# Three neighbouring chunks in one load: regrouping the cache loads of a two-layer decode kernel

## The chip, the cores and the metric

The kernel runs on one core of a Trainium2 chip. The metric is the device time of one execution in microseconds (us). Three runs of the kernel before gave 2494.72, 2493.18 and 2493.18 us, a median of 2493.18 us.

## What is computed

The reference is one decode step (one token for each of B = 2 sequences, D = 512 channels) through two layers that share all their weights and caches:

```python
x = x + A(layernorm(x))   # attention over a cache of 32768 tokens, 32 query heads on 8 KV heads, Dh = 128
x = x + B(layernorm(x))   # token mixer: W2 gelu(W1 layernorm(X)^T), with F = 1792 hidden values
x = x + A(layernorm(x))   # the same K and V caches a second time
x = x + B(layernorm(x))
```

For each sequence and KV head, four query rows are multiplied with 32768 keys, a softmax is taken, and its weights are multiplied with 32768 values. Everything is in 32-bit floats. K and V of both sequences are 537 MB, and each layer needs all of it, while the on-chip memory that the kernel uses for it holds about 28 MB. The second layer's queries of a sequence depend on the whole first layer of that sequence, the mixer included.

## The kernel before

**Units, chunks, cells.** A unit is one (layer, sequence, KV head): 32 units, numbered 0 to 31 in the order of the list `units`. K and V of a unit are cut into 8 chunks each (c0 to c7) of 4096 tokens. A chunk is 128 partitions by 4096 floats, 16 KB in each partition and 2 MB in all. One tile, `mem`, holds 13 cells of this size (0 to 12) and a rest of 5/8 of a cell (called cell 13). Chunks c0 to c3 of a unit, and c4 to c7, lie next to each other in every row of DRAM, so that one load can take several neighbouring chunks, with rows of 16 KB times their number. Far from the layer changes four chunks come in a load (64 KB rows) and the eight cells 0 to 7 are used in two groups of four.

**The order of the work.** The list `stream` (L858 to L869) sorts all loads by a key, so that K chunks of unit n+1 alternate with V chunks of unit n. The final loop (L1008) goes through it: it issues the load, then emits the matmuls of each chunk (`k_chunk`, L422: 16 instructions in two halves of 8; `v_chunk`, L567: the same), then the small work that was booked with `at(step, ...)` for this step. A step is one chunk; half steps (`vend + 0.5`) lie between the two halves of a chunk. TensorE (PE) executes in exactly this order. All cache and weight loads are issued by SyncE (its queue, SPq), in order: a load waits there until the last reader of its cells has finished, and every load behind it waits too. A matmul waits until the whole load that brought its chunk has landed.

**Which cell.** The choice is made when the program is built. `hold` notes until which step a cell is in use, `room` and `fit` say how many cells' worth of loads were issued since its last reader, and `spread` takes the cell with the most room; where there is less than two it cuts the chunk into two half loads of 1 MB (8 KB rows), for which `half` takes half cells with a room of at least one.

**What stays.** Head 7 (the `keeper`) is processed in layer 0 and layer 1 of a sequence without a second load of all of it: `KEPT_K` and `KEPT` name the K chunks (c0 to c2) and V chunks (c1 to c7, of c4 only 5/8, and two more eighths in PSUM) that layer 0 leaves in cells of their own until layer 1 has read them. So when a sequence changes from layer 0 to layer 1, the chunks kept can be worked on without a load. Units 13 (layer 0, sequence 0, head 7; N1) and 16 (layer 0, sequence 1, head 7; N2) are loaded into these cells; units 15 and 18 (N3) read them again. Units 14 and 17 (head 5 of the other sequence) run in between.

**A layer change.** After the last V chunk of unit 13 (or 16; its end is `vend`) comes a chain of small work: `out_0` (VectorE adds the blocks of `acc`), `out_1` and `out_2` (PE, L607 and L240), `take_rows`, `mix_2` (PE, L653), `hidden_sum` (14 gelu tiles on ScalarE, 14 sums on VectorE), `mix_3` (PE, L817), `to_columns`, and then the query products of the next unit. `mix_1` (PE, L629) is booked one step before `vend`. Meanwhile the loads go on with K chunks c2 to c7 of unit 14 (17), then V c0 and on. Nearly all cells are held by then, so these come as half loads in a ring of four half cells: the first half of c4 goes where the first half of c2 was, the first half of c5 where that of c3 was, the second halves likewise.

**Weights.** `load_weights` (L113) brings `wq` and `wo` of one head, 2 MB in 16 KB rows, into one of the cells 9 to 12, ten steps ahead of the first unit that needs them: 8 loads in layer 0, 6 in layer 1 (head 5 and 7 stay).

The functions that the change touches, with their lines:

Of the kernel before, what the change touches and what calls it, by code (L numbers as in the profile page):

```python
# [13 lines left out]
P = 128  # L14
CK = 4096
JT = CK // P
NG = 4
# [4 lines left out]
LAG = 1  # L22


KEPT_K = {0: 0, 1: 1, 2: 9}
KEPT = {1: (8, 6), 2: (8, 2), 3: (8, 11), 4: (5, 13), 5: (8, 3), 6: (8, 4), 7: (8, 5)}
REST = 5
IN_PSUM = (4, 5, 2)
KEPT_Q = 4
RESIDENT = (5, 7)  # L30
PAIRS = (2, 4, 7)
EVEN = 6
PIECES = (32, 16, 8, 4, 4)
THIN = 16
QT = 4
# [7 lines left out]
def gqa_mixer_kernel(ctx: ExitStack, tc: tile.TileContext, x, kt, v, wqo, cols, out):  # L43
# [20 lines left out]
    DH = D // NG  # L64
    NCH = kt.shape[1] // (CK * DH)
    HKV = U // B
    R = wqo.shape[2] // (2 * D)
    DT = D // P
    FT = (cols.shape[1] - 1) // 4
    LAYERS = 2  # L70
# [22 lines left out]
    nc.scalar.dma_start(xcols, x)  # L93


    W = wqo.shape[2] // 2
    assert CK == 2 * W
    WCELL0, WCELLS = RING * RING, 4
    heads = list(range(HKV))
# [10 lines left out]
    def wo_at(h):  # L110
        return cells(home[h])[:, W:].rearrange("p (t c) -> p t c", t=R)

    def load_weights(h, cell):  # L113
        home[h] = cell
        nc.sync.dma_start(cells(cell), wqo[h])


    busy = [0] * 2 * (WCELL0 + WCELLS + 1)
# [19 lines left out]

    def buffer(m, limit, until):

        ks = range(0, limit - m + 1, m) if limit != EVEN else [k + j for k in PAIRS for j in range(0, 2, m)]
        k = min(ks, key=lambda k: (-room(k, m, until), idle(k, m)) if limit == NCH else idle(k, m))
        assert idle(k, m) <= now[0]
        hold(k, m, until)
        return cells(k, m)
# [7 lines left out]

    def fit(k, m, until):

        return 0 if until > closed.get(int(k), until) else room(k, m, until)

    def room(k, m, until):

# [4 lines left out]

        return sum(brings[int(-(-a // 1)) : b])

    def spread(until, parted=False):

        k = min((*range(WCELL0 + 1), KEPT[3][1]), key=lambda k: (-fit(k, 1, until), idle(k)))
        if fit(k, 1, until) >= 2 and not parted:  # L170
            hold(k, 1, until)
            return [cells(k)]
        return [half(until - 0.5), half(until)]

    def quads(a):
# [213 lines left out]
    def load_k(n, c, m, limit):  # L389
        layer, b, h = unit_of(n)  # L390
        stay = h == keeper and c in KEPT_K
        own = KEPT_K[c] if stay else None
        until = k_done[n, c + m - 1]
        if own is not None:
            if stay and not layer:
                until = k_done[units.index((1, b, h)), c + m - 1]
            hold(own, m, until)
            bufs = [cells(own, m)]
        elif limit == RING:
            bufs = spread(until, n in (N1 + 1, N2 + 1) and c > 1)  # L400
# [89 lines left out]
    def load_v(n, c, m, limit):  # L490
        layer, b, h = unit_of(n)
        src = piece(v, b * HKV + h, c, m)
        stay, own = stays(n, c)
        until = v_done[n, c + m - 1]
        w = QT * DH
        f = stay * w
        at = quads(own) if stay else []
        if stay:
            if layer == 0:
                load(own, src[:, :f])  # L500
                for j in range(2 if stay > QT else 1):
                    busy[2 * KEPT[c][1] + j] = v_done[units.index((1, b, h)), c]
            if stay == JT // QT:
                v_at[n, c] = at
                return
            bufs = [half(until)[:, : CK - f]]
        elif limit == RING:
            bufs = spread(until)
# [47 lines left out]
    def v_chunk(n, c, part):  # L556
# [7 lines left out]
        for q in range(part * NG, min(quads, (part + 1) * NG)):  # L564
            g = q % NG
            col = (c2 * (JT // QT) + q) * 32 + a * R * QT
            nc.tensor.matmul(  # L567
                acc[32 * g : 32 * g + R * QT, :],
                S[half][:, col : col + R * QT],
                vc[q],  # L570
                start=(c == 0 and q < NG),
                stop=(c == NCH - 1 and q >= quads - NG),
            )
        if part < SUB - 1:
# [283 lines left out]
    stream = []  # L858
    for n in range(NU):
        stream += [(n * NCH + c + m - 1, 0, n, c, m, limit) for c, m, limit in parts(n, 0)]  # L860
        for c, m, limit in parts(n, 1):
            if n in (N1, N2):
                key = (n + 1) * NCH + 1 + (c + 1) / (2 * NCH)
            elif n in (N1 + 1, N2 + 1):
                key = (n + 1) * NCH - 0.5 + max(c / (2 * NCH) - 0.5, c - 1)
            else:
                key = (n + 1) * NCH + c + m - 1 + (LAG if N1 < n <= N3 else 0)
            stream.append((key, 1, n, c, m, limit))
    stream.sort()  # L869

# [13 lines left out]
        done.setdefault(time, []).append((rank, f, a))  # L884

    HC = NCH // HALVES
    weight_cell = {h: WCELL0 + h % WCELLS for h in heads}
    again = dict(zip(passing, (WCELL0 + k for k in (0, 2, 3, 1, 0, 2))))
    mixed = {}
    for n in range(NU):  # L890
        layer, b, h = unit_of(n)
# [3 lines left out]
        if n:  # L895
# [3 lines left out]
                place = S[1]  # L899
            else:  # L900
                place = S[0] if n in (N2 + 1, N3 + 1) else None
                q0 = kbeg[n] - (10 if n == N3 + 1 else 6)
# [5 lines left out]
            at(q2, make_q, n, 2, place)  # L908
            at(q3, make_q, n, 3, rank=int(q3 == q2))
            if place is S[0]:  # L910
                assert v_done[n - 2, HC - 1] <= q2
        if n and (units[n] == (0, 0, h) or h in passing and units[n] == (1, 0, h)):
            at(kbeg[n] - 10, load_weights, h, (again if layer else weight_cell)[h])
        if n in (N1 + 1, N2 + 1):
            at(kend - 0.5, turn_scores, n, 0, rank=2)
            at(kend, q_products, n + 1, 0)
# [10 lines left out]
            assert t1 + 1 < v_done[n, HC] - 1  # L927
        else:
            t1 = max(kend + 2, ahead + (2 if urgent else 4))
            at(kend + 1, max_1, n)  # L930
            at(kend + 2, max_2, n)
            t0 = max(k_done[n, HC - 1], v_done[n - 1, HC - 1] if n else 0)
# [53 lines left out]
        for j in range(2 * k, 2 * k + m):  # L986
            booked.setdefault(j, []).append(time)

    for n in (N1, N2):
        for c in KEPT_K:  # L990
            book(KEPT_K[c], 2, k_done[n, c] - 1)
        for c in KEPT:
            book(KEPT[c][1], 2 if KEPT[c][0] > QT else 1, v_done[n, c] - 1)
# [3 lines left out]
    closed[WCELL0], closed[WCELL0 - 1] = kbeg[N2 + 1], kbeg[N3 + 2] - 8  # L997
    closed[6] = closed[7] = kbeg[N3 + 2] - 10
    first_input()
    for step in range(4):  # L1000
        make_q(0, step)
# [20 lines left out]
def _layout(A_x, A_k_cache, A_v_cache, A_wq, A_wo, B_w1, B_b1, B_w2, B_b2):  # L1022
# [18 lines left out]
    wo = A_wo.reshape(HKV, -1, DH, D).transpose(0, 2, 1, 3)  # L1041
    w2 = B_w2.reshape(P, -1)
    w2 = np.stack([np.zeros_like(w2), w2], axis=2)
    cols = [a.reshape(P, -1) for a in (B_w1, B_b1, w2)] + [np.broadcast_to(B_b2.reshape(1, 1), (P, 1))]
# [32 lines left out]
```

## Time and profile before

| what | value |
|---|---|
| profiled execution | 2493.41 us, of which the span of the trace is 2491.6 us |
| PE matmul busy | 1378.2 us (55% of the span) |
| VectorE, ScalarE, GpSimd busy | 240.1, 187.8 and 4.9 us |
| bytes read from DRAM | 1061.7 MB, 426 GB/s over the span |
| granted TensorE clock, mean | 0.769 |

All times of the trace are in us from the start of the span. A row of a timeline gives the start, the duration, the engine, the source line, the operation, what it writes and reads with the shape, and the number of instructions that were merged; in square brackets stands how long the engine had been idle before and what ended that wait. "DMA share" is the mean busy share of the 16 DMA engines. The DMA rows give the size of a load and the time from its issue on SPq to its landing. The trace shows two PE matmul instructions for each matmul of the program (4096 on L422, where the loops make 2048).

### The profile page before, as it was taken

Reading aid. Unit: us, or ns where it says so; the run is one execution under the profiler, and the core shown is the slowest. Engines: PE = TensorE matmul, PEld = TensorE weight load, DVE = VectorE, ACT = ScalarE, POOL = GpSimd, SP = SyncE. Lnnn points to the kernel's source line nnn. Section 1 sums busy time; section 2 is a strip of 40 time slices with the busy share of each in tenths; the row PEclk is TensorE's granted clock in tenths of the full one; section 3 lists DMA queues with packets and bytes.
Section 4 is the critical chain, followed back from the end, with each engine's and each line's share of the span. In section 5 each row is a group of like instructions: output and inputs, shape, how many; then the busy total and the mean of one; then the engine's idle time right before and its main releaser. Section 6 shows DMA issues by size and latency. Waiting matters only on the chain.

```text
span 2491.6 us, 20496 instructions
## 1 busy us (share of the span) xinstructions
PE 1378.2 (55%) x9270; PEld 368.8 (15%) x9270; DVE 240.1 (10%) x632; ACT 187.8 (8%) x554; POOL 4.9 (0%) x17
## 2 busy tenths in 40 slices
PE   4544554655445454666677775464546555455546
PEld 1111111111111111111111111111111111111112
DVE  1000000000000000003113110000000000010002
ACT  0000000000000000002012010000000000011002
POOL 0000000000000000000000000000000000000000
PEclk8677767777777777878798787677777777777778
DMA  9999999999999999999999999999999999999996
GB/s 421 436 429 427 439 433 431 435 435 427 431 435 432 432 428 431 431 426 408 427 427 421 426 429 438 427 436 436 431 431 431 429 431 432 434 432 430 433 436 286
DMA packets 34080, 1063.04 MB, mean 427 GB/s; under 512 B 4037, under 2 KB 4041, under 8 KB 4938
## 3 DMA queue, kind: packets, MB, share of 16 engines
q1 hardware_dynamic: 33704, 1061.70, 99.2%
q8 instruction: 73, 1.20, 0.2%
q14 instruction: 13, 0.11, 0.0%
q10 hardware_dynamic: 290, 0.04, 0.0%
HBM read 1061.72 MB, written 0.00 MB: 426 GB/s over the span
## 4 chain that ended last, share of the span: by engine, by line
DMA 75%; PE 24%; issue 0%; DVE 0%; ACT 0%; SPq 0%; POOL 0%
DMA mem<-in_kt_dram 38%; DMA mem<-in_v_dram 37%; PE scores L422 11%; PE acc L567 10%; PE kept L334 1%; PE rows L240 0%; PE bcast L334 0%; PE small L607 0%; PE small L451 0%; PE small L598 0%; PE kept L749 0%; PE small L445 0%; PE bcast L817 0%; ACT S L462 0%; SPq L136 0%
## 5 line engine op out<-in xcount | busy, mean ns | idle before, releaser
L422 PE MATMUL scores<-mem,small_sb 128*32 128x512 f32 x4096 | 629.4, 732 | 608.7 <-DMA mem<-in_kt_dram 608.4
L567 PE MATMUL acc<-mem,S 128*16 128x512 f32 x4088 | 613.3, 736 | 460.3 <-DMA mem<-in_v_dram 457.9
L422 PEld LDWEIGHTS scores<-mem,small_sb 128*32 128x32 f32 x4096 | 147.8, 128 | 1001.0 <-issue 898.8
L462 ACT ACTIVATE S<-S,small_sb 128x128 f32<-128x128 f32 x240 | 123.5, 518 | 2104.4 <-DVE small_sb L453 1630.4
L567 PEld LDWEIGHTS acc<-mem,S 128*16 128x16 f32 x4088 | 133.2, 110 | 823.5 <-issue 674.7
L437 DVE TENSOR_REDUCE small_sb<-scores 128x1 f32<-128x512 f32 x64 | 44.2, 690 | 831.4 <-PE scores L422 831.4
L457 DVE STREAM_TRANSPOSE S<-scores 128x512 f32<-128x512 f32 x64 | 45.4, 710 | 124.0 <-PE acc L567 124.0
L334 PE MATMUL kept<-mem,small_sb 128*2 128x512 f32 x104 | 51.2, 619 | 1.7 <-DVE small_sb L268 1.7
L240 PE MATMUL rows<-mem,small_sb 128*1 128x512 f32 (+1 forms) x276 | 47.1, 601 | 2.6 <-ACT mem L792 2.4
L462 ACT ACTIVATION_READ_ACCUMULATOR S<-S,small_sb 128x1 f32 x240 | 44.8, 187 | 0.0
L447 DVE TENSOR_REDUCE small_sb<-small 1x4 f32<-1x128 f32 x32 | 8.9, 279 | 276.5 <-PE small L445 276.5
L600 DVE RECIPROCAL small_sb<-small 128x4 f32<-128x4 f32 x32 | 5.9, 184 | 291.4 <-PE small L598 291.4
L609 DVE TENSOR_TENSOR small_sb<-small,small_sb 128x4 f32<-128x4 f32 x31 | 5.1, 164 | 291.6 <-PE small L607 291.6
L537 DVE SCALAR_TENSOR_TENSOR S<-acc,small_sb,S 128x128 f32<-128x128 f32 x93 | 32.6, 351 | 3.3
L792 ACT ACTIVATE S<-bcast,small_sb 128x512 f32<-128x512 f32 x28 | 21.6, 777 | 92.4 <-DVE small_sb L661 90.3
L535 DVE TENSOR_SCALAR S<-acc,small_sb 128x128 f32<-128x128 f32 x31 | 10.8, 349 | 158.9 <-PE acc L567 158.9
L360 PE MATMUL small<-small_sb,mem 2*128 2x2 f32 x112 | 14.7, 249 | 17.9 <-DVE mem L356 17.9
L607 PEld LDWEIGHTS small<-small_sb,S 128*128 128x128 f32 x62 | 13.0, 262 | 46.0 <-issue 40.0
L334 PE MATMUL bcast<-mem,small_sb 128*1 128x512 f32 (+1 forms) x40 | 19.1, 592 | 0.0
L809 DVE SCALAR_TENSOR_TENSOR acc<-S,small_sb,acc 128x512 f32<-128x512 f32 x24 | 18.1, 755 | 2.5
L360 PEld LDWEIGHTS small<-small_sb,mem 2*128 2x128 f32 x112 | 13.5, 186 | 30.5 <-DVE mem L356 27.3
L607 PE MATMUL small<-small_sb,S 128*128 128x4 f32 x62 | 15.7, 323 | 1.7 <-DVE S L537 1.7
(134 smaller groups left out, 265.5 us busy)
## 6 DMA issues: line engine op xcount, KB each, us to landing
mem<-in_kt_dram SPq DMA_DIRECT2D x32, 2048.0 KB, 16.5
mem<-in_v_dram SPq DMA_DIRECT2D x23, 2048.0 KB, 20.9
mem<-in_v_dram SPq DMA_DIRECT2D x9, 4096.0 KB, 27.1
mem<-in_wqo_dram SPq DMA_DIRECT2D x14, 2048.0 KB, 33.5
mem<-in_kt_dram SPq DMA_DIRECT2D x7, 4096.0 KB, 23.7
mem<-in_kt_dram SPq DMA_DIRECT2D x24, 1024.0 KB, 8.8
mem<-in_v_dram SPq DMA_DIRECT2D x21, 1024.0 KB, 8.4
mem<-in_v_dram SPq DMA_DIRECT2D x2, 1280.0 KB, 26.5
```

What stands on the lines that cost most here:

```text
L240: nc.tensor.matmul(rows[32 * g : 32 * g + b + 1, :], weights if b else weights[:, 1:], row, start=False, stop=True, skip_group_check=True,)
L334: nc.tensor.matmul(q_ps[n][:m, :], xnT[:, d, b : b + m], wq_at(h)[:, d, :], start=(d == 0), stop=(d == DT - 1),)
L360: nc.tensor.matmul(pt[:, r * m : (r + 1) * m], q_row[n][:m, r * DH : (r + 1) * DH], ident[:m, :m], start=True, stop=True,)
L422: nc.tensor.matmul(sc_ps[n, half][32 * g : 32 * g + 32, :], q, kc[k * NG + g], start=(i == 0 and k == 0), stop=(i == PACK - 1 and k == SUB ...
L437: nc.vector.tensor_reduce(mx[n][:, half : half + 1], sc_ps[n, half], axis=AX.X, op=ALU.max)
L457: nc.vector.transpose(S[half], sc_ps[n, half])
L462: nc.scalar.activation(s[:, :, h], s[:, :, h], AF.Exp, bias=neg[n][:, h : h + 1], scale=SCALE, accum_out=lsum[n][:, half, h : h + 1],)
L537: nc.vector.scalar_tensor_tensor(t, acc[:, k * DH : (k + 1) * DH], mask[:, k : k + 1], t, op0=ALU.mult, op1=ALU.add)
L567: nc.tensor.matmul(acc[32 * g : 32 * g + R * QT, :], S[half][:, col : col + R * QT], vc[q], start=(c == 0 and q < NG), stop=(c == NCH - 1 ...
L607: nc.tensor.matmul(po[:, :R], row_tile()[:, :DH], selh, start=True, stop=True)
L792: nc.scalar.activation(hid[key, f], px[key], AF.Gelu_apprx_tanh, bias=shift[key][:, f : f + 1], scale=slope[key][:, f : f + 1],)
L809: nc.vector.scalar_tensor_tensor(h if f == FT - 1 else acc, h, w, acc, op0=ALU.mult, op1=ALU.add)
```

## The change

The same bytes are loaded, in other groups and partly other cells.

- V c1 to c3 of units 13 and 16 come in one load of 6 MB (48 KB rows) into cells 8, 9, 10, and V c5 to c7 in one into cells 3, 4, 5; before, each chunk had its own load. K c0 to c2 of these units come in one load into cells 0, 1, 2.
- Near the changes some K and V chunks come in pairs: K c4 and c5, c6 and c7 of units 13 and 16 (in unit 13 they were pairs before), K c0 and c1 of units 14 and 17, all K pairs of unit 19, and all of these, and V of unit 12, take their cells from `spread`, which now handles several cells (`RING_CELLS`).
- `load_weights` brings two heads in a load (32 KB rows, two cells): 7 loads for 14. The pair of heads 0 and 1 for layer 1 is booked seven steps ahead of unit 20 rather than ten, and goes to cells 9 and 10, which V c2 and c3 of unit 18 have held until then.
- V of unit 15 is ordered by a list (`FOLLOWS`): its kept chunks c1 to c3 come first, c0 after them. The maxima and exponentials of units 14 to 18 that are not at a change are booked up to two steps earlier (`e`).
- Work booked at half steps is run inside loads of several chunks too.

```diff
-KEPT_K = {0: 0, 1: 1, 2: 9}
-KEPT = {1: (8, 6), 2: (8, 2), 3: (8, 11), 4: (5, 13), 5: (8, 3), 6: (8, 4), 7: (8, 5)}
+KEPT_K = {0: 0, 1: 1, 2: 2}
+KEPT = {1: (8, 8), 2: (8, 9), 3: (8, 10), 4: (5, 13), 5: (8, 3), 6: (8, 4), 7: (8, 5)}
+RING_CELLS = 11
+PLACE_V = {(1, 7): 1, (5, 0): 2}
...
-PAIRS = (2, 4, 7)
-EVEN = 6
+TWO_HEADS = ((0, 1), (2, 3), (4, 6), RESIDENT)
+FOLLOWS = (2.2, -0.9, -0.8, -0.7, 3.5, 3.6, 3.7, 5.5)
...
-    def load_weights(h, cell):
-        home[h] = cell
-        nc.sync.dma_start(cells(cell), wqo[h])
+    def load_weights(k, cell):
+        for j in range(2):
+            home[TWO_HEADS[k][j]] = cell + j
+        nc.sync.dma_start(cells(cell, 2), wqo[k])
...
-    def spread(until, parted=False):
-
-        k = min((*range(WCELL0 + 1), KEPT[3][1]), key=lambda k: (-fit(k, 1, until), idle(k)))
-        if fit(k, 1, until) >= 2 and not parted:
-            hold(k, 1, until)
-            return [cells(k)]
+    def spread(m, until, parted=False, place=None):
+
+        ks = range(RING_CELLS - m + 1) if place is None else [place]
+        k = min(ks, key=lambda k: (-fit(k, m, until), idle(k, m)))
+        if fit(k, m, until) >= 2 and not parted:
+            hold(k, m, until)
+            return [cells(k, m)]
+        assert m == 1
         return [half(until - 0.5), half(until)]
...
+        if stay and m > 1:
+            k = KEPT[c][1]
+            own = cells(k, m)
+            load(own, src)
+            for j in range(m):
+                hold(k + j, 1, v_done[units.index((1, b, h)), c + j])
+                v_at[n, c + j] = quads(cells(k + j))
+            return
...
-        if m == N1:
-            loads = ((0, 2), (2, 2), (4, 2), (6, 2)) if with_v else ((0, 2), (2, 1), (3, 1), (4, 2), (6, 2))
-            return [(c, k, EVEN) for c, k in loads]
-        return [(c, 1, EVEN if n == N1 + 1 and not with_v and c < 2 else RING) for c in range(NCH)]
+        if not with_v:
+            loads = ((0, 3), (3, 1), (4, 2), (6, 2)) if n in (N1, N2) else ((0, 2), (2, 2), (4, 2), (6, 2))
+            if n in (N1 + 1, N2 + 1):
+                loads = ((0, 2), *((c, 1) for c in range(2, NCH)))
+            if n in (N1 + 2, N3):
+                loads = [(c, 1) for c in range(NCH)]
+        elif n in (N1, N2):
+            loads = ((0, 1), (1, 3), (4, 1), (5, 3))
+        elif n in (N1 + 1, N2 + 1):
+            loads = [(c, 1) for c in range(NCH)]
+        elif n < N1:
+            loads = ((0, 2), (2, 2), (4, 2), (6, 2))
+        else:
+            loads = [(c, 1) for c in range(NCH)]
+        return [(c, k, RING) for c, k in loads]
...
+            elif n == N1 + 2:
+                key = (n + 1) * NCH + FOLLOWS[c]
...
-            at(kbeg[n] - 10, load_weights, h, (again if layer else weight_cell)[h])
+        if n and h in opens and (units[n] == (0, 0, h) or h in passing and units[n] == (1, 0, h)):
+            at(kbeg[n] - (7 if n == N3 + 2 else 10), load_weights, opens[h], WCELL0 + opens[h] % 2 * 2)
...
-            at(kend + 1, max_1, n)
-            at(kend + 2, max_2, n)
+            e = kend if N1 < n <= N3 else kend + 2
+            at(max(kend, e - 1), max_1, n)
+            at(e, max_2, n)
...
-            at(kend + 2, exponentials, n, 0)
+            at(e, exponentials, n, 0)
...
-                if m == 1 and part == 0:
+                if part == 0:
                     run(t + 0.5)
...
-        "wqo": np.concatenate([wq.reshape(HKV, P, -1), wo.reshape(HKV, DH, -1)], axis=2),
+        "wqo": np.stack([np.concatenate([wqo[h] for h in two], axis=1) for two in TWO_HEADS]),
```

More of the change, by code (lines that the diff above doesn't have):

```diff
@@ L66, in gqa_mixer_kernel @@
     HKV = U // B
-    R = wqo.shape[2] // (2 * D)
+    R = wqo.shape[2] // (4 * D)
     DT = D // P
@@ L93, in gqa_mixer_kernel @@
     nc.scalar.dma_start(xcols, x)
-    W = wqo.shape[2] // 2
+    W = wqo.shape[2] // 4
     assert CK == 2 * W
@@ L139, in buffer @@
     def buffer(m, limit, until):
-        ks = range(0, limit - m + 1, m) if limit != EVEN else [k + j for k in PAIRS for j in range(0, 2, m)]
-        k = min(ks, key=lambda k: (-room(k, m, until), idle(k, m)) if limit == NCH else idle(k, m))
+        k = min(range(0, limit - m + 1, m), key=lambda k: (-room(k, m, until), idle(k, m)))
         assert idle(k, m) <= now[0]
@@ L154, in fit @@
     def fit(k, m, until):
-        return 0 if until > closed.get(int(k), until) else room(k, m, until)
+        shut = any(until > closed.get(j, until) for j in range(int(k), int(-(-(k + m) // 1))))
+        return 0 if shut else room(k, m, until)
     def room(k, m, until):
@@ L391, in load_k @@
         stay = h == keeper and c in KEPT_K
-        own = KEPT_K[c] if stay else None
         until = k_done[n, c + m - 1]
[L394 to L398, printed above, removed]
+        if stay:
+            for j in range(m):
+                hold(KEPT_K[c + j], 1, k_done[units.index((1, b, h)), c + j])
+            bufs = [cells(KEPT_K[c], m)]
         elif limit == RING:
-            bufs = spread(until, n in (N1 + 1, N2 + 1) and c > 1)
+            bufs = spread(m, until, n in (N1 + 1, N2 + 1) and m == 1)
         else:
@@ L497, in load_v @@
         at = quads(own) if stay else []
+        if stay and m > 1:
+            k = KEPT[c][1]
+            own = cells(k, m)
+            load(own, src)
+            for j in range(m):
+                hold(k + j, 1, v_done[units.index((1, b, h)), c + j])
+                v_at[n, c + j] = quads(cells(k + j))
+            return
         if stay:
@@ L507, in load_v @@
         elif limit == RING:
-            bufs = spread(until)
+            bufs = spread(m, until, False, PLACE_V.get((n - N1, c)))
         else:
@@ L570, in v_chunk @@
                 vc[q],
-                start=(c == 0 and q < NG),
+                start=(c == (n == N1 + 2) and q < NG),
                 stop=(c == NCH - 1 and q >= quads - NG),
@@ L864, in gqa_mixer_kernel @@
             elif n in (N1 + 1, N2 + 1):
-                key = (n + 1) * NCH - 0.5 + max(c / (2 * NCH) - 0.5, c - 1)
+                key = (n + 1) * NCH - 0.5 + max(c / (2 * NCH) - 0.5, c - 2 + m)
+            elif n == N1 + 2:
+                key = (n + 1) * NCH + FOLLOWS[c]
             else:
-                key = (n + 1) * NCH + c + m - 1 + (LAG if N1 < n <= N3 else 0)
+                key = (n + 1) * NCH + c + m - 1 + (LAG if N1 - 1 <= n <= N3 else 0)
             stream.append((key, 1, n, c, m, limit))
@@ L886, in gqa_mixer_kernel @@
     HC = NCH // HALVES
-    weight_cell = {h: WCELL0 + h % WCELLS for h in heads}
-    again = dict(zip(passing, (WCELL0 + k for k in (0, 2, 3, 1, 0, 2))))
+    opens = {two[0]: k for k, two in enumerate(TWO_HEADS)}
     mixed = {}
@@ L901, in gqa_mixer_kernel @@
                 place = S[0] if n in (N2 + 1, N3 + 1) else None
-                q0 = kbeg[n] - (10 if n == N3 + 1 else 6)
+                q0 = kbeg[n] - (10 if n == N3 + 1 else 4 if n == N3 + 2 else 6)
                 q1, q2, q3 = q0 + 1, q0 + 2, q0 + 2
@@ L910, in gqa_mixer_kernel @@
             if place is S[0]:
-                assert v_done[n - 2, HC - 1] <= q2
-        if n and (units[n] == (0, 0, h) or h in passing and units[n] == (1, 0, h)):
-            at(kbeg[n] - 10, load_weights, h, (again if layer else weight_cell)[h])
+                assert max(v_done[n - 2, c] for c in range(HC)) <= q2
+        if n and h in opens and (units[n] == (0, 0, h) or h in passing and units[n] == (1, 0, h)):
+            at(kbeg[n] - (7 if n == N3 + 2 else 10), load_weights, opens[h], WCELL0 + opens[h] % 2 * 2)
         if n in (N1 + 1, N2 + 1):
@@ L929, in gqa_mixer_kernel @@
             t1 = max(kend + 2, ahead + (2 if urgent else 4))
-            at(kend + 1, max_1, n)
-            at(kend + 2, max_2, n)
-            t0 = max(k_done[n, HC - 1], v_done[n - 1, HC - 1] if n else 0)
+            e = kend if N1 < n <= N3 else kend + 2
+            at(max(kend, e - 1), max_1, n)
+            at(e, max_2, n)
+            t0 = max(k_done[n, HC - 1], *(v_done[n - 1, c] for c in range(HC) if n), 0)
             if n in (N2, N3):
@@ L987, in book @@
             booked.setdefault(j, []).append(time)
[L989 to L993, printed above, removed]
+    for t0, (_, is_v, n, c, m, _) in zip(starts, stream):
+        if n in (N1, N2) and c in (KEPT if is_v else KEPT_K):
+            for j in range(m):
+                if is_v:
+                    book(KEPT[c + j][1], 2 if KEPT[c + j][0] > QT else 1, t0)
+                else:
+                    book(KEPT_K[c + j], 2, t0)
+    hold(WCELL0, 2, v_done[N1 - 2, NCH - 1] + 3)
     first = next(t for t, (*_, n, _, m, limit) in zip(starts, stream) if n > N3 and m == PACK)
@@ L996, in gqa_mixer_kernel @@
         book(k, 2 * PACK, first + k)
-    closed[WCELL0], closed[WCELL0 - 1] = kbeg[N2 + 1], kbeg[N3 + 2] - 8
-    closed[6] = closed[7] = kbeg[N3 + 2] - 10
+    closed[WCELL0] = closed[WCELL0 + 1] = kbeg[N2 + 1]
+    closed[WCELL0 - 1] = kbeg[N3 + 2] - 8
     first_input()
@@ L1041, in _layout @@
     wo = A_wo.reshape(HKV, -1, DH, D).transpose(0, 2, 1, 3)
+    wqo = np.concatenate([wq.reshape(HKV, P, -1), wo.reshape(HKV, DH, -1)], axis=2)
     w2 = B_w2.reshape(P, -1)
```

## The prediction

> **What bounds the kernel now.** I read the page first: the span, the DMA queues, the chain that ended last, the DMA issues.
>
> ```profile
> span 2491.6 us, 20496 instructions
> ...
> q1 hardware_dynamic: 33704, 1061.70, 99.2%
> ...
> DMA 75%; PE 24%; issue 0%; DVE 0%; ACT 0%; SPq 0%; POOL 0%
> ...
> mem<-in_kt_dram SPq DMA_DIRECT2D x32, 2048.0 KB, 16.5
> mem<-in_v_dram SPq DMA_DIRECT2D x23, 2048.0 KB, 20.9
> mem<-in_v_dram SPq DMA_DIRECT2D x9, 4096.0 KB, 27.1
> mem<-in_wqo_dram SPq DMA_DIRECT2D x14, 2048.0 KB, 33.5
> ```
>
> The loads' queue (q1) fills the 16 DMA engines for 99.2% of the span, and the chain is DMA for three quarters. So the kernel lasts as long as its bytes take, and a change can act in two ways only: through the rate at which bytes move, or through moments in which the queue is empty. The bytes stay the same. The size table gives the loads in question: 14 of weights, and 32 + 23 = 55 of single chunks.
>
> Then I asked for the rate in four stretches, each within one kind of load: single chunks with 16 KB rows, half chunks with 8 KB rows, pairs with 32 KB rows, fours with 64 KB rows; and for two microseconds at the first layer change. The last two columns are DMA share and GB/s.
>
> ```profile
> 1203.00:1268.00 65.00, 42.24 (x256) 8.83 (x256) 7.08 (x18) 4.13 (x16) 0.00 (x0) 0.77 1.01 428
> 1334.00:1368.00 34.00, 24.39 (x138) 5.09 (x130) 19.67 (x39) 13.48 (x18) 1.08 (x2) 0.90 1.01 421
> 1486.00:1552.00 66.00, 39.92 (x236) 9.59 (x236) 2.69 (x9) 3.12 (x12) 0.00 (x0) 0.77 1.00 430
> 1600.00:1740.00 140.00, 69.91 (x475) 19.27 (x472) 9.58 (x28) 6.47 (x24) 0.00 (x0) 0.76 1.00 433
> 1180.00:1182.00 2.00, 2.00 (x21) 0.79 (x13) 0.49 (x1) 0.00 (x0) 0.00 (x0) 1.00 0.77 291
> ```
>
> The engines are full in the first four; longer rows only move a little more in the same time: 421 GB/s for 8 KB, 428 for 16, 430 for 32, 433 for 64. At 1180 the queue ran empty for a moment (share 0.77, 291 GB/s).
>
> **Term 1, longer rows: -2.1 us.** Going through `parts` and `load_weights`, the change turns 14 weight loads into 7 pairs, and of the 55 single chunks it keeps 23; the other 32 become 7 pairs and 6 triples. So 14 + 32 = 46 chunks of 2.097 MB, 96.5 MB, leave the 16 KB rows, 28 of them for 32 KB and 18 for 48 KB. The 45 half loads stay. At 428 GB/s 96.5 MB take 225.4 us, at 432 GB/s (between the rows for 32 and 64 KB) 223.3 us. Bounds: 428 to 430 gives -1.1 us, 428 to 433 gives -2.6 us.
>
> 26 loads fewer are issued. A half load that met an empty queue took 5.4 us from issue to landing (row below), while one in the stream takes 1.05 MB / 421 GB/s = 2.5 us of the engines. The 2.9 us between are hidden as long as another load is queued, which the shares of 1.00 and 1.01 say. The Trainium skill (DMA: Bandwidth & Descriptors, Anatomy of one DMA) puts the time of a DMA at about 2.0 us plus its bytes at 436 GB/s; by that, 26 loads fewer would save 52 us. The traced shares speak against it, since they leave no such gaps.
>
> **Term 2, the two layer changes: +6.7 us.** Three chunks in one load land together, when the last of them would have landed. V c5 to c7 of unit 13 are what the whole layer change waits for. PE's rows there, before:
>
> ```profile
> 1133.77 3.26 PE L567 MATMUL acc<-mem,S 128*16 128x512 f32 x16 [3.86 <-DMA mem<-in_v_dram]
> 1138.66 1.91 PE L567 MATMUL acc<-mem,S 128*16 128x512 f32 x16 [1.63 <-DMA mem<-in_v_dram]
> 1140.50 1.16 PE L629 MATMUL bcast<-small_sb 128*128 128x128 f32 x8
> 1143.57 1.91 PE L567 MATMUL acc<-mem,S 128*16 128x512 f32 x16 [1.91 <-DMA mem<-in_v_dram]
> 1146.06 1.06 PE L422 MATMUL scores<-mem,small_sb 128*32 128x512 f32 x8 [0.58 <-DMA mem<-in_kt_dram]
> 1147.11 0.39 PE L607 MATMUL small<-small_sb,S 128*128 128x4 f32 x2
> 1148.55 1.06 PE L422 MATMUL scores<-mem,small_sb 128*32 128x512 f32 x8 [1.05 <-DMA mem<-in_kt_dram]
> 1149.43 1.04 PE L240 MATMUL rows<-mem,small_sb 128*1 128x512 f32 x8
> 1151.29 1.12 PE L653 MATMUL bcast<-S,small_sb 128*128 128x512 f32 x2 [0.81 <-DVE S L621]
> ```
>
> c5, c6, `mix_1` and c7 are worked off one by one as they land, and after the last landing (1143.57) only c7's 1.91 us remain: `acc` is complete at 1145.48. After the change all four follow that landing: 3.26 (c5 after a long wait runs slow, as in the first row) + 1.91 + 1.16 + 1.91 = 8.24 us, to 1151.8. The first half of K c2 of unit 14 comes next on PE: 1.06 us, to 1152.9, where it ended at 1147.1 before.
>
> That half holds the place for the first half of K c4, and SPq waits for it with everything behind. What cover there is, the issues of half loads show, from issue to landing: K c4's first half issued at 1147.2; K c5's, issued at 1153.5; and one issued at 1180.7, when the queue had run empty.
>
> ```profile
> mem<-in_kt_dram SPq DMA_DIRECT2D x1, 1024.0 KB, 8.7
> ...
> mem<-in_kt_dram SPq DMA_DIRECT2D x1, 1024.0 KB, 7.4
> ...
> mem<-in_v_dram SPq DMA_DIRECT2D x1, 1024.0 KB, 5.4
> ```
>
> So c4's issue can come 8.7 - 5.4 = 3.3 us later at no cost, and c5's 7.4 - 5.4 = 2.0. c4's comes 1152.9 - 1147.2 = 5.7 us later: the queue is dry for 2.4. c5's waits for the first half of K c3, which PE takes after `out_1`, the second half of K c2, `out_2` and `mix_2`. From `acc` complete to `out_1` were 1.63 us (1145.48 to 1147.11), then 0.39; from the second half of c2 to the end of `mix_2` 3.86 (1148.55 to 1152.41). So 1151.8 + 1.63 + 0.39 + 3.86 + 1.06 = 1158.7 and issue at 1158.8, 5.3 late, 3.3 beyond its cover. The two lie on one queue, so the larger counts: **+3.3 us**. The chain behind (`hidden_sum` to `mix_3`) moves by about as much as the loads do, and isn't charged again.
>
> The second change has the same rows 189 us later:
>
> ```profile
> 1332.94 1.91 PE L567 MATMUL acc<-mem,S 128*16 128x512 f32 x16
> ...
> 1345.47 1.07 PE L422 MATMUL scores<-mem,small_sb 128*32 128x512 f32 x8 [1.51 <-DMA mem<-in_kt_dram]
> ...
> L136 SPq DMA_DIRECT2D mem<-in_kt_dram x1: 328/328/328, 1336.6 to 1336.6; - x1
> ...
> mem<-in_kt_dram SPq DMA_DIRECT2D x1, 1024.0 KB, 7.5
> ```
>
> c4's first half, issued at 1336.6, was waited for until 1345.4, 8.8 us; c5's (issued at 1342.8) took 7.5. With the same 8.24 us from 1332.94, `acc` is complete at 1341.2, K c3's first half at 1348.1, 5.4 late against a cover of 2.1: **+3.3 to +3.4 us**. Bounds for each change: nothing, if the ring has cover that these rows don't show; 6.3 us, the whole delay of `acc`, if it has none.
>
> V c1 to c3 in one load cost nothing: their cells wait for nobody soon, and PE has the transfer of c4 to c7, four chunks of 4.9 us, to catch up. The first weights, 4 MB in place of 2 ahead of the first K load, only reorder bytes. K c0 to c2 of unit 16 need cell 1, which V c7 of unit 14 leaves with two chunks (9.8 us) still queued.
>
> **Term 3, the weight pair in layer 1: +2.4 us.** It goes into cells 9 and 10, so SPq holds it until PE is through V c2 and c3 of unit 18. One head's load before went into a cell long free. PE's rows near there, before:
>
> ```profile
> 1428.09 3.41 PE L422 MATMUL scores<-mem,small_sb 128*32 128x512 f32 x16 [0.73 <-DMA mem<-in_kt_dram]
> ...
> 1462.45 3.30 PE L422 MATMUL scores<-mem,small_sb 128*32 128x512 f32 x16 [6.25 <-DMA mem<-in_kt_dram]
> ```
>
> K c7 of unit 18 lands at 1428.05. Then follow K c0-1 of unit 19 (9.7 us for a pair), V c0 (4.9), K c2-3, K c4-5: landings at 1437.8, 1442.7, 1452.4 and 1462.1, and then the weights. PE's order is K c2, K c3, V c2, V c3 from 1452.4 on: 3.30, then three times 1.91 as above, 9.0 in all, to 1461.4. Issued then into a queue nearly empty, 4 MB land 5.4 + 3.15 MB / 432 GB/s = 12.7 us later, at 1474.1; without a gap it would be 1471.8. Bounds: nothing if PE is a little quicker, 4.5 us if it is 2 us slower.
>
> **Sum.** -2.1 + 3.3 + 3.4 + 2.4 = +7.0 us. The profiled execution took 2493.41 us, 1.8 over its span; the median of the runs is 2493.18. I predict 2493.2 + 7.0 = **2500.2 us**, 0.28% more. The earlier maxima and exponentials, the order of unit 15's V and the half-step work change what PE and ScalarE do while loads are queued; I charge nothing.
>
> **Rivals.**
> *The cover holds.* If the delay of `acc` at either change stays under what is queued, and PE frees cells 9 and 10 before 1459, only term 1 is left: 2491.1 us, not slower. It decides from a cover of 5.4 us for K c5's issue; the rows say 2.0 and 2.1. For it speaks that these rest on one landing at an empty queue. Chance 17%; 8% that just one of the three places costs (2493 to 2496).
> *The mixer chain becomes the bound.* If `acc` comes later than 6.3 us, or PE, colder, takes longer to `mix_3`, V c0 of unit 14 is late too, and the queue, which ran dry at 1180 before, runs dry for the whole delay of 6 us or more at each change: 2493.2 - 2.1 + 12 + 2.4 = 2505.5 us and up. Against it: the loads move back by 3.3 us themselves. Chance 10%.
> *Each load saved saves its own overhead.* 26 x 2.9 us would be 75 us, to 2418; but 1061.7 MB at the best stretch's 433 GB/s need 2452, so at most that and the ends. The full DMA shares speak against it; faster by over 0.2% in any way gets 5%. The Trainium skill's 52 us (the page above) would give 2441 us.
>
> **How the numbers follow.** My forecast, two dry changes and a late weight pair (2496 to 2505), has 60%. 0.2% is 5.0 us, about what a measurement of this kernel can tell from no change: slower begins at 2498.2. Three quarters of the forecast and the second rival lie beyond: 55%. Within: a quarter of the forecast, the first rival and its neighbours, 40%. Faster 5%. The range reaches from the first rival's 2490.5 to 2506.
>
> **What the profile after would show.** At the changes PE's L567 rows as one run of 48 (with L629) after a wait of ten us, ending some 6 us after the landing; half loads of K c4 with 5.4 us from issue to landing; GB/s in the stretch near 1150 to 1160 and 1340 to 1350 clearly under 421; SPq waiting for `acc` ahead of the weights of layer 1. Single-chunk stretches that became pairs at 430 and over. Wrong would be: half loads still at 7 to 9 us, or dry stretches elsewhere, above all before K c0 to c2 of unit 16.

## The result, and the profile after

The changed kernel takes 2501.99 us (median of 6 runs, 2499.47 to 2504.80), the kernel before 2493.45 us (median of 6, 2493.18 to 2494.72). The ratio is 1.0034, with a 95% interval of 1.0021 to 1.0047: 8.5 us slower. Predicted were 2500.2 us, within 2490.5 to 2506.0. The profiled execution is the quickest of the six, 2499.47 us with a span of 2497.7 us, 6.1 us above the profiled one of before; what the others lost beyond that, no trace shows.

The page of the profile after, the rows that answer to those of before:

```profile
span 2497.7 us, 20458 instructions
...
q1 hardware_dynamic: 29960, 1061.70, 98.8%
...
mem<-in_kt_dram SPq DMA_DIRECT2D x14, 4096.0 KB, 21.9
mem<-in_v_dram SPq DMA_DIRECT2D x9, 4096.0 KB, 29.1
mem<-in_wqo_dram SPq DMA_DIRECT2D x7, 4096.0 KB, 37.7
mem<-in_kt_dram SPq DMA_DIRECT2D x12, 2048.0 KB, 20.9
mem<-in_v_dram SPq DMA_DIRECT2D x4, 6144.0 KB, 31.7
```

The same 1061.70 MB go in fewer packets (29960 for 33704), and the queue fills less of the span, 98.8 for 99.2%: it ran empty more. Where, four stretches show, first of the kernel before, then of the changed one: the first layer change, V c2 of unit 14, the second change, the weights of layer 1 (the last three columns are the granted TensorE clock, the DMA share and GB/s).

```profile
1140.00:1160.00 20.00, 12.75 (x92) 3.15 (x84) 8.33 (x19) 4.69 (x7) 0.55 (x1) 0.95 0.99 392
1180.00:1190.00 10.00, 7.25 (x68) 2.32 (x64) 4.25 (x7) 0.63 (x1) 0.00 (x0) 1.00 0.95 383
1340.00:1350.00 10.00, 5.32 (x34) 0.96 (x34) 7.30 (x14) 5.32 (x7) 0.54 (x1) 1.00 1.01 421
1450.00:1470.00 20.00, 13.18 (x104) 3.34 (x107) 2.77 (x5) 0.00 (x0) 0.00 (x0) 0.83 1.01 427
```

```profile
1140.00:1160.00 20.00, 14.82 (x108) 4.21 (x108) 5.05 (x14) 1.37 (x2) 0.55 (x1) 0.87 0.79 311
1180.00:1190.00 10.00, 8.96 (x68) 2.50 (x66) 5.11 (x9) 1.26 (x2) 0.00 (x0) 1.00 0.99 401
1340.00:1350.00 10.00, 8.41 (x72) 2.33 (x68) 4.49 (x13) 0.26 (x1) 0.54 (x1) 1.00 0.82 306
1450.00:1470.00 20.00, 13.27 (x110) 3.86 (x109) 2.77 (x5) 0.00 (x0) 0.00 (x0) 0.83 0.85 353
```

A share of 0.79 in 20 us is 4.2 us without a transfer, 0.82 in 10 is 1.8, 0.85 in 20 is 3.0. All three were full before. The small gap at 1180 us shrank from 0.5 to 0.1.

The windows at the two changes are of unequal length, and the second begins when part of the loss has passed (1330 to 1340 us: 386 GB/s, 414 before). Over 60 us around each change, first of the kernel before, then of the changed one, the loss is alike:

```profile
1120.00:1180.00 60.00, 40.40 (x234) 8.69 (x226) 21.15 (x42) 13.49 (x18) 1.09 (x2) 0.86 1.00 413
1310.00:1370.00 60.00, 42.91 (x249) 9.42 (x241) 21.82 (x43) 13.49 (x18) 1.08 (x2) 0.84 1.01 421
```

```profile
1120.00:1180.00 60.00, 39.98 (x249) 9.82 (x250) 20.54 (x41) 12.87 (x17) 1.09 (x2) 0.76 0.94 389
1310.00:1370.00 60.00, 39.88 (x246) 9.67 (x246) 20.32 (x40) 12.87 (x17) 1.08 (x2) 0.75 0.96 397
```

24 GB/s less for 60 us are 3.5 us at the first change and 3.4 us at the second, at the rates of before; windows of 80 us (1100 to 1180, 1300 to 1380) give 3.3 and 3.0. At the weights, 401 in place of 429 GB/s from 1440 to 1480 us are 2.6 us.

PE's rows at the two changes, with the row of the weights' issue, say why:

```profile
1142.51 4.95 PE L578 MATMUL acc<-mem,S 128*16 128x512 f32 x32 [9.59 <-DMA mem<-in_v_dram]
1147.40 1.16 PE L640 MATMUL bcast<-small_sb 128*128 128x128 f32 x8
1148.48 1.91 PE L578 MATMUL acc<-mem,S 128*16 128x512 f32 x16
1150.21 1.04 PE L425 MATMUL scores<-mem,small_sb 128*32 128x512 f32 x8
...
1333.60 4.98 PE L578 MATMUL acc<-mem,S 128*16 128x512 f32 x32 [9.55 <-DMA mem<-in_v_dram]
1338.51 1.16 PE L640 MATMUL bcast<-small_sb 128*128 128x128 f32 x8
1339.60 1.91 PE L578 MATMUL acc<-mem,S 128*16 128x512 f32 x16
...
1456.15 5.16 PE L425 MATMUL scores<-mem,small_sb 128*32 128x512 f32 x32 [5.54 <-DMA mem<-in_kt_dram]
1461.14 3.61 PE L578 MATMUL acc<-mem,S 128*16 128x512 f32 x32
...
1464.82 0.33 SPq L118 DMA_DIRECT2D mem<-in_wqo_dram  x1
```

PE waits 9.6 us for the triple, and then has c5, c6, `mix_1` and c7 before it: `acc` is complete 7.9 us after the landing (1142.51 to 1150.39, and 1333.60 to 1341.51), where 1.91 us were enough before: 6.0 us late, counted from the landing. The weights are issued 0.07 us after V c3 of unit 18 (1461.14 + 3.61).

The first half loads of K c4 at the two changes (issues between 1150 and 1153, and between 1342 and 1344 us) met an empty queue, 4.9 and 4.6 us from issue to landing, where 8.7 and 8.8 us were usual:

```profile
mem<-in_kt_dram SPq DMA_DIRECT2D x1, 1024.0 KB, 4.9
...
mem<-in_kt_dram SPq DMA_DIRECT2D x1, 1024.0 KB, 4.6
```

### The profile page after: what moved, and what is told of

The parts are those of the page before. It is cut to its first block, busy times and chain, and to the rows that moved or that the text cites. A ratio compares the mean times of both kernels' runs of the same rounds, so it can differ in the third digit from the quotient of the medians.

```text
span 2497.7 us, 20458 instructions
## 1 busy us (share of the span) xinstructions
PE 1363.6 (55%) x9270; PEld 369.5 (15%) x9270; DVE 240.2 (10%) x632; ACT 187.7 (8%) x554; POOL 4.9 (0%) x17
## 3 DMA queue, kind: packets, MB, share of 16 engines
q1 hardware_dynamic: 29960, 1061.70, 98.8%
## 4 chain that ended last, share of the span: by engine, by line
DMA 75%; PE 24%; another core or an unknown queue 0%; issue 0%; DVE 0%; ACT 0%; SPq 0%
DMA mem<-in_v_dram 66%; PE acc L578 19%; DMA mem<-in_kt_dram 9%; PE scores L425 3%; PE small L454 0%; PE small L609 0%; PE bcast L339 0%; PE rows L245 0%; PE small L448 0%; PE kept L760 0%; PE bcast L664 0%; PE bcast L640 0%; DVE S L548 0%; ACT mem L770 0%
## 5 line engine op out<-in xcount | busy, mean ns | idle before, releaser
L578 PE MATMUL acc<-mem,S 128*16 128x512 f32 x4088 | 601.3, 726 | 474.5 <-DMA mem<-in_v_dram 472.1
L803 ACT ACTIVATE S<-bcast,small_sb 128x512 f32<-128x512 f32 x28 | 21.6, 778 | 101.5 <-DVE small_sb L672 99.4
```

Source lines behind the costliest of these rows:

```text
L578: nc.tensor.matmul(acc[32 * g : 32 * g + R * QT, :], S[half][:, col : col + R * QT], vc[q], start=(c == (n == N1 + 2) and q < NG), stop=(c ...
L803: nc.scalar.activation(hid[key, f], px[key], AF.Gelu_apprx_tanh, bias=shift[key][:, f : f + 1], scale=slope[key][:, f : f + 1],)
```

## The experiments

The theory is the prediction's: the last triple makes PE late and the ring of half cells runs dry (term 2), SPq waits with the weights (term 3), longer rows give a little (term 1). All medians stand beside the kernel before, run on the same chip. "Against before" is the difference of the medians, in brackets the 95% interval of the ratio.

| run | us | before, us | against before |
|---|---|---|---|
| the changed kernel | 2501.99 | 2493.45 | +8.5 (1.0021 to 1.0047) |
| last_single | 2494.83 | 2493.69 | +1.1 (0.9995 to 1.0012) |
| weights_later | 2500.80 | 2493.69 | +7.1 (1.0018 to 1.0039) |
| pair_and_later | 2491.97 | 2493.69 | -1.7 (0.9984 to 1.0002) |
| triple_alone | 2501.83 | 2493.69 | +8.1 (1.0022 to 1.0049) |
| delay_3 | 2494.81 | 2493.64 | +1.2 (0.9998 to 1.0015) |
| delay_6 | 2498.28 | 2493.64 | +4.6 (1.0008 to 1.0026) |
| kept_warm | 2500.73 | 2493.64 | +7.1 (1.0017 to 1.0039) |
| kept_warm_41 | 2498.90 | 2494.34 | +4.6 (1.0007 to 1.0025) |
| short_rows | 2515.26 | 2493.64 | +21.6 (1.0072 to 1.0103) |
| first_single | 2501.55 | 2494.34 | +7.2 (1.0022 to 1.0047) |

**last_single.** The changed kernel without the last triple.

```diff
         elif n in (N1, N2):
-            loads = ((0, 1), (1, 3), (4, 1), (5, 3))
+            loads = ((0, 1), (1, 3), (4, 1), (5, 1), (6, 1), (7, 1))
```

> The changed kernel with V c5, c6 and c7 of units 13 and 16 in a load each; all else, the weight pairs too, as changed. Theory (the last triple lands late, PE falls 6 us behind and the ring of half cells runs dry): the 3.7 and 1.9 us of empty queue that the trace after shows at the two changes go, single rows cost 0.2 us back, the weights' 2.5 us stay: 2502.0 - 5.4 = 2496.6 us, and K c4's first half has 8 to 9 us from issue to landing again. Rival 1 (the weight pair makes the whole loss): 2502 us as changed. Rival 2 (loads of several cells cost by themselves, wherever they are): a part, about 0.5 of 8.5 us, 2501.5 us.

Measured were 2494.83 us: from +8.5 to +1.1 against before. One load at each change holds nearly all of the loss, and both rivals fall. 7.4 us come back where 5.4 were expected: the expectation took 1.9 us for the second change, and the bytes above give 3.4. In the trace the first change is almost full again, the second is full, K c4's first half takes 7.8 us from issue to landing, and the weights' gap stays (0.84 of 20 us):

```profile
1140.00:1160.00 20.00, 12.83 (x84) 3.42 (x84) 8.57 (x19) 4.94 (x7) 0.54 (x1) 0.91 0.96 377
1340.00:1350.00 10.00, 5.61 (x41) 0.82 (x40) 7.25 (x14) 6.59 (x9) 0.54 (x1) 1.00 1.02 419
1450.00:1470.00 20.00, 14.94 (x110) 3.86 (x110) 2.58 (x4) 0.00 (x0) 0.00 (x0) 0.83 0.84 347
```

**triple_alone.** The other way round: only this triple, in the kernel before, where the cells 3, 4, 5 lay side by side already.

```diff
+        if with_v and n in (N1, N2):
+            return [(c, m, RING) for c, m in ((0, 1), (1, 1), (2, 1), (3, 1), (4, 1), (5, 3))]
         return [(c, 1, EVEN if n == N1 + 1 and not with_v and c < 2 else RING) for c in range(NCH)]
```

(and in `load_v` the branch for several kept chunks, as in the change.)

> The kernel before with one thing of the change: V c5 to c7 of units 13 and 16 in one load into the same cells 3, 4, 5. Theory: the changes cost what they cost in the changed kernel, 3.7 and 1.9 us in its trace, 3.3 and 3.4 in the prediction: 2493.4 + 5.6 to 6.7 = 2499 to 2500 us. Rival 1 (the weights make the whole loss): 2493.4 us. Rival 2 (the new cells or the new order of other loads are needed for the loss): 2493 to 2495 us.

Measured were 2501.83 us, 8.1 more than before: the triple alone costs as much as the whole change. That is 1.4 to 2.5 us more than expected. In its trace the two changes lose 3.6 and 2.7 us by the windows of 60 us (388 and 402 GB/s), and the queue runs dry a third time, behind the mixer of the second change, first in the kernel before, then here:

```profile
1370.00:1380.00 10.00, 7.89 (x70) 2.70 (x74) 3.90 (x7) 0.63 (x1) 0.00 (x0) 1.00 1.00 411
```

```profile
1370.00:1380.00 10.00, 10.00 (x56) 2.86 (x52) 3.69 (x10) 0.63 (x1) 0.00 (x0) 0.85 0.87 345
```

66 GB/s less are 1.6 us. PE begins V c0 of unit 17 at 1376.08, 40.5 us after it began c5 of the triple; before it was 35.1 us after it began c7 (1332.94 to 1368.07), and in the changed kernel's trace 38.5. That trace has no such gap (410 GB/s); first_single's has it (338 GB/s; an execution of 2505.36 us), and so has kept_warm_41's (349). Whether the slower executions of the changed kernel have it too, no trace shows.

**weights_later.** The changed kernel, with the weights for unit 20 issued where their cells are free.

```diff
-            at(kbeg[n] - (7 if n == N3 + 2 else 10), load_weights, opens[h], WCELL0 + opens[h] % 2 * 2)
+            at(kbeg[n] - (3 if n == N3 + 2 else 10), load_weights, opens[h], WCELL0 + opens[h] % 2 * 2)
...
-                q0 = kbeg[n] - (10 if n == N3 + 1 else 4 if n == N3 + 2 else 6)
+                q0 = kbeg[n] - (10 if n == N3 + 1 else 2 if n == N3 + 2 else 6)
```

> The changed kernel with the weight pair for unit 20 issued behind K c6-7 of unit 19 instead of K c4-5 (three steps ahead of the unit, its query products two steps ahead), where cells 9 and 10 are long free. Theory (SPq waits for V c2 and c3 of unit 18): the 2.5 us of empty queue near 1465 us go, all else stays: 2502.0 - 2.5 = 2499.5 us. Rival 1 (the weights make the whole loss): 2493 us. Rival 2 (that wait is hidden in the executions that aren't profiled): 2502 us.

Measured were 2500.80 us, +7.1 for +8.5 against before. The gap at 1460 us is gone from the trace, and the first rival falls; but 1.4 us is less than the 2.5 expected, and the intervals overlap, so this run alone doesn't tell the theory from the second rival. The trace of this execution has more time without a transfer at the layer changes (shares of 0.74 and 0.78, for 0.79 and 0.82):

```profile
1140.00:1160.00 20.00, 16.02 (x108) 4.40 (x108) 4.49 (x13) 0.23 (x1) 0.54 (x1) 0.81 0.74 290
1340.00:1350.00 10.00, 8.41 (x68) 2.79 (x64) 3.36 (x8) 0.00 (x0) 0.00 (x0) 1.00 0.78 301
1450.00:1470.00 20.00, 13.95 (x114) 3.96 (x110) 2.77 (x5) 0.00 (x0) 0.00 (x0) 0.91 1.01 430
```

**pair_and_later.** Both mended, but with c5 and c6 as a pair:

```diff
-            loads = ((0, 1), (1, 3), (4, 1), (5, 3))
+            loads = ((0, 1), (1, 3), (4, 1), (5, 2), (7, 1))
```

(and the two lines of weights_later.)

> The changed kernel with V c5-6 of units 13 and 16 as a pair and c7 alone, and the weights later as in the run before. Theory: after c7's landing PE has only c7 left, and c6 and mix_1 overlap with its transfer, so acc is complete at most 1.5 us later than in the kernel before, inside the cover of 3.3 and 2.0 us; all empty stretches go but that of 0.5 us at the first change, and the longer rows are left: 2493.4 - 2.1 = 2491.3 us, faster than both. Rival 1 (a pair there is already too late): 2494 to 2497 us. Rival 2 (loads of several cells cost by themselves): 2493.5 us or more.

Measured were 2491.97 us (2491.12 to 2494.12, 11 runs), 10.0 under the changed kernel and 1.7 under the one before; this last difference is not told from none, as the interval reaches to 1.0002, and with it the second rival isn't quite excluded. The first is, by the trace: the pair lands 4.6 us ahead of where the triple did, PE goes through c5, c6, `mix_1` and c7 without a wait, and `acc` is complete at 1146.13, 0.65 us later than in the kernel before.

```profile
1137.88 5.32 PE L578 MATMUL acc<-mem,S 128*16 128x512 f32 x32 [5.09 <-DMA mem<-in_v_dram]
1143.13 1.16 PE L640 MATMUL bcast<-small_sb 128*128 128x128 f32 x8
1144.22 1.91 PE L578 MATMUL acc<-mem,S 128*16 128x512 f32 x16
```

Against last_single, on the same chip, 2.9 us are gained; the two differ in the weights' place and in two pairs for four single chunks (0.1 us by the rates). So by these medians the weights' wait costs nearer 2.8 us where the changes don't stall; the bytes in the changed kernel's trace gave 2.6.

**delay_3 and delay_6.** No load is touched; PE alone is made late, in the kernel before.

```diff
             at(vend - 1 if change else vend, mix_1, key)
+            if change:
+                at(vend - 0.5, idle_products, 10)
```

(20 in delay_6.)

> The kernel before with ten unread products of the identity matrix (some 2.9 us of PE) between the halves of V c7 of units 13 and 16: no load is changed, acc is complete 2.9 us later at each layer change. Theory (the ring of half cells covers a late PE up to a point): K c4's issue comes some 2.3 us late against a cover of 3.3, K c5's 1.9 late against 2.0, so next to nothing: 2493.7 to 2494.7 us. Rival (no cover, or the mixer chain is the bound, so that each us of PE counts): 2493.7 + 5.8 = 2499.5 us.

> The same with twenty products, 5.8 us, close to the 6 us by which the triple makes acc late. Theory: K c5's issue is 4.8 us late against a cover of 2.0, 2.8 us of empty queue at each change: 2493.7 + 5.6 = 2499.3 us, and with the 8.1 us of the triple alone in mind up to 2501. If the landing of three chunks had a cost beside PE's lateness, this run stays well under that one: 2496 us or less. Rival (the mixer chain is the bound): 2493.7 + 11.6 = 2505 us.

Measured were +1.2 and +4.6 us; the first can't be told from none, as its interval begins at 0.9998. In the traces the products make `acc` 2.55 and 4.8 us late at the first change (V c7 ends at 1147.87 and 1150.14; its halves alone would have ended at 1145.32 and 1145.35), and as late at the second. In triple_alone, counted from the landing, it was 6.8 and 6.2 us late. So there are three points for the loss over both changes: 2.55 late costs 1.2, 4.8 costs 4.6, 6.2 to 6.8 costs 8.1, of which 1.6 lie in the third stretch. By the bytes of the 60 us windows, delay_6 loses 2.3 and 2.1 us: about 2.5 us of its lateness are free. PE's lateness is enough to make a loss of this size. The 1.4 and 2.0 us by which the triple is later still, taken one for one, bring 4.6 to 8.0, so it needs no cost of its own; the intervals would hide one of a us or two. The rivals fall: the first us are covered, and the later ones don't count doubly. PE's rows of delay_6 at the first change, and the two stretches, in which the queue runs dry as in the changed kernel:

```profile
1143.44 1.05 PE L567 MATMUL acc<-mem,S 128*16 128x512 f32 x8
1144.42 4.73 PE L697 MATMUL small<-small_sb 128*128 128x128 f32 x40
1149.09 1.05 PE L567 MATMUL acc<-mem,S 128*16 128x512 f32 x8
```

```profile
1140.00:1160.00 20.00, 17.34 (x132) 8.32 (x128) 5.24 (x14) 1.48 (x3) 0.54 (x1) 0.93 0.86 341
1340.00:1350.00 10.00, 8.41 (x67) 2.36 (x69) 4.49 (x13) 0.53 (x1) 0.54 (x1) 1.00 0.86 321
```

**kept_warm and kept_warm_41.** The changed kernel, with unread products for PE in the wait for the triple.

```diff
             at(vend - 1 if change else vend, mix_1, key)
+            if change:
+                at(v_done[n, 4], idle_products, 30)
```

(41 in the second.)

> The changed kernel with thirty unread products (some 8.7 us) on PE behind V c4 of units 13 and 16, in the ten us in which PE waits for the last triple. Theory (the wait makes the first chunk after it slow, 3.1 to 3.6 us in place of 1.9): acc is complete 1.2 to 1.7 us earlier at each change, and that much less of the queue is empty: 2502 - 2.4 to 3.4 = 2499 us. Rival (what counts is the order of the work, not PE's speed): 2502 us. If the products last beyond the landing, as long again is lost.

> The changed kernel with 41 unread products behind V c4 in place of the 30 of the run before, which lasted 6.96 us and left PE idle again for 3.7 and 2.6 us; 41 take 9.5 us and reach nearly to the landing of the last triple. Theory (a PE that didn't wait runs c5 in 1.9 in place of 3.1 us): acc is complete 1.2 us earlier at each change, 2502 - 2.4 = 2499.6 us, and the rows for c5 and c6 together show 3.8 us in place of 5.0. Rival (PE's speed doesn't matter): 2502 us.

Thirty products lasted only 6.96 us; PE was idle again for 3.7 and 2.6 us, and c5 and c6 took 5.3 and 5.1 us, no less than before. So the +7.1 of this run says nothing on the theory. With 41 the two take 3.63 us at both changes:

```profile
1132.96 9.42 PE L708 MATMUL small<-small_sb 128*128 128x128 f32 x82
1142.48 3.63 PE L578 MATMUL acc<-mem,S 128*16 128x512 f32 x32
...
1321.38 9.42 PE L708 MATMUL small<-small_sb 128*128 128x128 f32 x82
1331.63 3.63 PE L578 MATMUL acc<-mem,S 128*16 128x512 f32 x32 [0.82 <-DMA mem<-in_v_dram]
```

and the loss falls from +8.5 to +4.6, 3.9 us less where 2.4 were expected; the intervals (5.2 to 11.7 and 1.7 to 6.2 us) allow either, and just overlap. By the medians, work that nobody reads makes the changed kernel quicker. In the trace the first change loses 1.9 in place of 3.5 us and the second 2.6 in place of 3.4 (400 and 403 GB/s in the windows of 60 us), but 1.5 us go behind the second mixer, where the changed kernel's trace lost none. PE's slowness after a wait is part of the loss, of a size that these runs leave open.

**short_rows.** Term 1 enlarged, in the kernel before: every load of four chunks in four.

```diff
     def load(t, src):
-        nc.sync.dma_start(t, src)
+        w = CK if t.shape[-1] == PACK * CK else t.shape[-1]
+        for i in range(0, t.shape[-1], w):
+            nc.sync.dma_start(t[:, i : i + w], src[:, i : i + w])
```

> The kernel before with each of its 95 loads of four chunks issued as four loads of one chunk into the same cells: 16 KB rows in place of 64 KB for 797 MB, 285 loads more, no byte more. Theory (rate by row length, 433 against 428 GB/s): 797 MB take 1862 in place of 1841 us: 2493.7 + 21 = 2515 us. Rival 1 (every load has about 2.0 us of its own that shows, as in the rule weighed in the prediction): 570 us more, 3060 us. Rival 2 (the length of the rows isn't what sets the rate): 2494 us.

Measured were 2515.26 us, +21.6 for the +21 worked out from two windows. The stretch that moved 433 GB/s moves 428, with the engines as full:

```profile
1600.00:1740.00 140.00, 85.99 (x478) 18.03 (x482) 9.57 (x28) 6.36 (x24) 0.00 (x0) 0.74 1.01 428
```

285 more loads cost 0.08 us each, which is what the rate of their rows accounts for. Nearly every load here has 128 rows, so shorter rows also mean more loads, and this run can't tell a rate set by the rows from 0.08 us that each load takes by itself.

**first_single.** The changed kernel with V c1, c2, c3 in single loads: `((0, 1), (1, 1), (2, 1), (3, 1), (4, 1), (5, 3))`.

> The changed kernel with V c1, c2 and c3 of units 13 and 16 in a load each, while c5 to c7 stay a triple. Theory (only the last triple makes PE late, since PE catches up with c1 to c3 while c4 to c7 move): as changed, 2502.0 us, plus 0.2 us for the shorter rows. Rival (a late landing of three chunks costs wherever it is): half of the loss at the changes goes, 2498 us.

Measured were 2501.55 us, as the changed kernel: the first triple costs nothing.

## Why the prediction was right

**Term 1 (-2.1 us): right.** pair_and_later has all the longer rows but those of two chunks and no dry stretch at the three places, and gains 1.7 us by the medians, an amount that its interval can't tell from none. short_rows shows the rate behind it on eight times the bytes: 21.6 us for 797 MB between 64 and 16 KB rows, so at most 2.6 us for the 96.5 MB here.

**The 26 loads fewer: right at nothing.** The rule of the Trainium skill that was weighed there (DMA: Bandwidth & Descriptors, Anatomy of one DMA), 2.0 us for each DMA, would make short_rows 570 us slower; it was 21.6. That section gives the rule for loads that GpSimd issues, while SyncE issues these. As long as other loads are queued, that part doesn't show here. What a load may cost by itself is the 0.08 us of short_rows: for 26 loads 2.0 us, which is term 1 by another name and not to be added to it.

**Term 2 (+6.7 us): the mechanism right, the size right in the profiled execution and some 1 us too small by the medians.** The order of PE after the landing is as worked out, 7.9 us for the predicted 8.24, and the bytes missing in the trace are 3.5 and 3.4 us, for the predicted 3.3 and 3.4. triple_alone measures 8.1 us for the two changes, with 1.6 in a third stretch that the sum doesn't have, and last_single takes 7.4 of the 8.5 us back. In part the agreement is luck, as two small errors offset each other. `acc` was put 6.3 us late and was 6.0. The cover, put at 2.0 us for K c5's issue, let about 3.0 us of that pass for nothing (6.3 late, 3.3 lost); the traces leave about 2.5 (6.0 late, 3.5 and 3.4 lost, and 4.8 late, 2.3 and 2.1 lost in delay_6). The floor of 5.4 us behind it was one landing; two others took 4.9 and 4.6, which should have made the cover larger, not smaller. What eats it isn't settled.

**Term 3 (+2.4 us): right in place, its size between 1.4 and 2.8 us by two comparisons of medians, 2.6 us by the bytes in the trace.** PE's order and the issue came as worked out: 33.4 us after the landing of K c7 of unit 18 by the prediction; in the trace after, PE begins that chunk as it lands, at 1431.09, and the issue is at 1464.82, 33.7 us later.

**The rivals.** The cover didn't hold. The mixer chain didn't become the bound in the changed kernel's trace, where the gap at 1180 us shrank; in triple_alone's it did in part, behind the second change (1.6 us). Saved loads saved nothing beside the 2 us of term 1. The remaining edits (the order of unit 15's V, the earlier exponentials, the first triple, the weights of layer 0) were charged nothing; pair_and_later, which keeps them all, isn't slower than before. The stretches that the prediction named as a sign of being wrong, dry ones elsewhere, don't show between the changes (1200 to 1300 us: share 1.01, 431 GB/s).

## What to carry to other kernels

A load of several tiles lands as one. Where a chain waits for the last tile, count what its consumer still has to do after that landing, the slow start after the wait included, and compare it with what is queued for the loads that wait for that consumer: here 6 us of lateness at each of two changes, against some 2.5 us of cover, cost 7 to 8 us in all, for rows that gave 2. Join the tiles ahead of the last, and let the last come alone.

A load that must wait for a reader holds everything behind it in its queue. Put it where its place has been free for as long as the queue is deep.

## What the runs showed of the hardware

- PE after a wait: 32 instructions of c5 and c6 took 4.95 and 4.98 us after 9.6 us idle, 3.63 after none or 0.8 us, and still 5.05 after 2.6 us of idle time, in the row of kept_warm below. The two rows behind it are the first 1.8 us of such work in kept_warm, at a granted clock of 0.50, and in kept_warm_41 after 0.8 us, at 1.00. The Trainium skill (TensorE: Matmul & The Clock Gate, Part 1: The HAM clock gate) puts the fall to half clock behind an idle window of about 3.4 us. The direction agrees; 2.6 us were enough here, so that figure is no safe bound for a wait.

```profile
1334.80 5.05 PE L578 MATMUL acc<-mem,S 128*16 128x512 f32 x32 [2.59 <-DMA mem<-in_v_dram]
...
1334.80:1336.60 1.80, 1.80 (x12) 0.43 (x16) 0.00 (x0) 0.00 (x0) 0.00 (x0) 0.50 1.00 414
...
1331.63:1333.40 1.77, 1.77 (x20) 0.52 (x24) 0.00 (x0) 0.00 (x0) 0.00 (x0) 1.00 1.01 421
```

- In the packet records of the trace after, the first packets of K c2, the half load behind the triple, begin 5.4 us before the last packet of the triple ends at the first change, and 1.9 us at the second. So the packets of neighbouring loads overlap in time, by amounts that differ from place to place. The two changes lost alike all the same (3.5 and 3.4 us), and no run varied the overlap.
